# Loading two weight blocks in runs of 1 KB instead of 14 and 7 KB

## The chip, the cores and the metric

The kernel runs on one core of one Trainium2 chip. The metric is device time in microseconds (us) of one execution. The host's work of laying out the inputs before the launch is not part of it. Five engines work side by side: TensorE (PE, matrix multiplications), VectorE (DVE), ScalarE (ACT), GpSimd (POOL) and SyncE (SP, which only issues transfers). Transfers are carried by 16 DMA engines that all queues share. In this kernel nearly all of them are issued by SP (the profile's queue q1); POOL issues some (queue q0), and ACT issues three.

## The reference

The input `A_u` is a sequence of 2048 tokens with 512 features, in bf16. After a layer normalisation the result is a sum of three parts: the input itself, a long convolution and a gated feed-forward block.

```python
xn = _layernorm(x, axis=-1)
return x + _A_ref(xn, ...) + _B_ref(xn, w_gate, w_up, w_down)

# _B_ref
g = jnp.einsum("bsd,df->bsf", x, w_gate)      # 512 -> 1792
u = jnp.einsum("bsd,df->bsf", x, w_up)        # 512 -> 1792
h = _sigmoid(g) * u
return jnp.einsum("bsf,fd->bsd", h, w_down)   # 1792 -> 512
```

`_A_ref` builds, for each of the 512 features, a kernel of length 2048 from 128 complex modes (powers of exp(dt*A), weighted by B and C). It convolves the sequence with it through Fourier transforms of length 4096, and adds the normalised input times `Dskip`.

## The kernel before, in words

The feed-forward block runs in four groups of 512 tokens (L1015). In each group there are 14 column blocks of 128 (`k`, L1021). For each block PE makes the gate product (`fg`, L1027) and the up product (`fu`, L1042) into PSUM banks; ACT takes the sigmoid of the gate (L1036), copies some of the up products to `us_sb` (L1053), and DVE multiplies the two into `hT_sb` (L1057). Then PE multiplies by the down weights (`fd`, L1086).

The convolution needs, first, a ladder of powers, W[0] to W[11], by repeated squaring (L649 to L665). In step k ACT squares both parts (L652), DVE makes the next power (L661, L663), and POOL copies the current power to bf16 with two DMAs (`f_cw`, L655 to L658). The next power is written into one of three buffers in turn. So step k must wait until the copy of step k - 2 has read its buffer (`W_op[-2:-1]`, L664). From the copies, tables of powers are made (`cmul`, lines L718 to L724; `squares`, L771 to L777; seeds copied at L291 or L293). The normalised input is transformed by matrix products (L680 and later). The third and fourth pieces of the input's normalisation take their statistics on ACT or DVE (L531 to L540) and one power function on POOL (L491). Normalised rows of the later groups go out to a scratch (`x_scr`, L568) and return transposed (L570).

The order of the work is written out by hand: `run` (L296) yields the operations in the order of `ORDER`. Each engine and each queue executes its share of that order one after another. The costs and `pkt` values that stand beside operations feed a planner (`_rate`, L306); with `ORDER` written out, they do not move anything.

The weights are loaded once, at the start, by SP, and stay in SBUF: `wg_sb` (gate), `wu_sb` (up) and `wd_sb` (down). By `ORDER`, SP issues at the start: rows 0 and 2 to 3 of the input, the first parameters, a gate piece, input rows 4 to 7, a gate piece, the other parameters, the last gate piece, the first up piece, input rows 12 to 15, the second up piece (L478 with n = 3), input rows 8 to 11, the small table S1 (L475) and the down weights (L484). Then SP comes to the store of the normalised rows 4 to 7 into `x_scr`, for which it waits. Loads on one queue are carried in the order of issue.

The host lays out what is loaded (`_laid_out`, L1149). In the kernel before, each of the 128 partitions finds its part of a weight piece in one run: 7168 bytes of an up piece, 14336 bytes of the down weights.

Of the kernel before, what the change touches and what calls it, by code (L numbers as in the profile page):

```python
# [20 lines left out]
D = 512  # L21
# [4 lines left out]
FT = 14  # L26
# [9 lines left out]
CUT_G = (0, 128, 3 * 128, 7 * 128, 14 * 128)  # L36
CUT_U = (0, 7 * 128, 14 * 128)
# [30 lines left out]
KB = 1024  # L68
# [255 lines left out]
def kernel(  # L324
# [27 lines left out]
    def slots(n):  # L352
        return [_Slot("b") for _ in range(n)]
# [16 lines left out]
    wu_sb = const.tile([128, KT * F], BF, name="wu_sb")  # L370
    wd_sb = const.tile([128, FT, D], BF, name="wd_sb")
# [15 lines left out]
    def at(off, shape, dt=BF):  # L387
        assert off % 32 == 0
        n = int(np.prod(shape)) * (4 if dt == F32 else 2)
        assert off + n <= NBIG, (off, n)  # L390
        v = big[:, off // 2:(off + n) // 2]
        if dt == F32:
            v = v.bitcast(F32)
        if len(shape) > 1:
            ax = ["a%d" % i for i in range(len(shape))]
            v = v.rearrange("p (%s) -> p %s" % (" ".join(ax), " ".join(ax)), **dict(zip(ax[1:], shape[1:])))
        return v
# [21 lines left out]
    def dma(q, dst, src, deps=(), prio=0.0, acq=(), rel=(), pkt=1024, after=None, hv=0.5):  # L419

        n = None
        get = lambda v: v() if callable(v) else v
        holder = {}

        def fn():
            with nc.allow_non_contiguous_dma(reason="laid out"):
                holder["i"] = QUEUE[q].dma_start(out=get(dst), in_=get(src))
            if after:
                after(holder["i"])

        return lambda nbytes: pl.add(q, 0.62, fn, deps, prio, acq, rel, dma=(nbytes, _rate(pkt), hv))
# [8 lines left out]
        return A_u[0:256, :].rearrange("(i p) d -> p i d", i=2)  # L440
    lp = [0.0]

    def load(q, dst, src, nbytes, deps=(), pkt=2048, hv=0.5):
        lp[0] += 0.01
        return dma(q, dst, src, deps=deps, prio=lp[0], pkt=pkt, hv=hv)(nbytes)

    def load_x(i0, n, q="SP"):
        ls = [load(q, xn[:, i0:i0 + n, :], xv(i0, i0 + n), 128 * n * KB,
                   pkt=1024 * n)]
        for i in range(i0, i0 + n):  # L450
            l_x[i] = ls
# [6 lines left out]
    ld, rawn = par[:, 0, :], {nm: par[:, 1 + qi, :] for qi, nm in enumerate(["Are", "Aim", "Bre", "Bim", "Cre", "Cim"])}  # L458
    l_id = None
    l_pa = load("SP", par[:, 0:3, :], A_par[:, 0:3, :], 384 * KB, pkt=3072)  # L460
    l_pbc = load("SP", par[:, 3:7, :], A_par[:, 3:7, :], 512 * KB, pkt=4096)
    l_wg, l_wu = [], []
    piece = lambda k: sum(128 * k >= c for c in CUT_G[1:-1])
# [6 lines left out]
    for n in range(4):  # L470
        fs_ = slice(KT * CUT_G[n], KT * CUT_G[n + 1])
        nb = 1024 * (CUT_G[n + 1] - CUT_G[n])
        l_wg.append(load("SP" if n else "ACT", wg_sb[:, fs_], B_w_gate[:, fs_], nb, pkt=nb // 128))
        if n == 2:
            l_s1 = load("SP", at(OFF["pq"], [128]), cten["S1"].ap(), 32 * KB)  # L475
        if n > 1:
            fs_ = slice(KT * CUT_U[n - 2], KT * CUT_U[n - 1])
            l_wu.append(load("SP", wu_sb[:, fs_], B_w_up[:, fs_], 896 * KB, pkt=7168))  # L478
        if n == 2:
            load_x(4, 4)  # L480
    load_x(8, 4)
    l_dk = load("SP", dskr[0:1, :], A_Dskip.rearrange("(o d) -> o d", o=1), 1 * KB)
    load_x(12, 4)
    l_wd = load("SP", wd_sb[:], B_w_down, 1792 * KB, pkt=14336)  # L484
    l_m2 = load("SP", m2[:], cten["M2"].ap(), 256 * KB, pkt=2048)
    l_sw = load("SP", sw[:], cten["SW"].ap(), 96 * KB, pkt=768)

# [242 lines left out]
    for c in range(4):  # L730
# [10 lines left out]
        n = 1  # L741
# [114 lines left out]
    for p, u2 in [(p, UNITS[p][n:n + 2]) for p in range(NP) for n in range(0, NU // 2, 2)]:  # L856
# [80 lines left out]
        for x, u in enumerate(u2):  # L937
# [6 lines left out]
                               pkt=512)(256 * KB))  # L944
# [34 lines left out]
    for t in range(0, 8, 2):  # L979
        lds = []  # L980
        for n, (p, u0, u1) in enumerate(VPART):
            v_v = v_scr[n][:].rearrange("g (a t r) d -> t (g a) (r d)", a=4, t=4)
            lds.append(dma("SP", vall[16 * u0:16 * u1, t // 2, p], v_v[t // 2],
                           deps=v_st[n] + table_free + z_free * p, prio=20 + n + 0.01 * t, pkt=2048, hv=0.9)(64 * KB * (u1 - u0)))
# [30 lines left out]
    for grp in range(4):  # L1015
        hts, prods = [], []
        for u2 in range(7):
# [3 lines left out]
            for k in (2 * u2, 2 * u2 + 1):  # L1021
                a, b = slots(2)
# [38 lines left out]
        for jj in range(4):  # L1061
# [3 lines left out]
            if jj == 0:  # L1065
                if late:
                    xt = at(TAIL["xt"], [4, D])
                    lx = [dma("SP", xt, xv(i, i + 4), deps=[prods[0]] + table_free, prio=3,
                              pkt=4096)(512 * KB)]
# [30 lines left out]
            if late:  # L1100
# [3 lines left out]
                for (c0, c1), po, my in zip(cols, pos, sums):  # L1104
# [4 lines left out]
                    if jj == 0:  # L1109
                        continue  # L1110
                    q0 = 0 if jj == 1 else r
                    src = lambda r=r, q0=q0, ot=ot, c0=c0, c1=c1: ot()[:, q0:r + 1, c0:c1]
                    dst = outv[:, i - r + q0:i + 1, c0:c1]
                    dma("ACT" if c0 else "SP", dst, src, deps=[fin], prio=1, rel=[osl] if r and c1 == 512 else [],
                        pkt=2 * (c1 - c0))(256 * (c1 - c0) * (r + 1 - q0))
# [23 lines left out]
def _rows(a):  # L1139
    return _swap(a.reshape(2, 32, 2, NT, D).transpose(2, 0, 1, 3, 4).copy()).reshape(128, NT, D)  # L1140
# [4 lines left out]
def _pieces(w, cut):  # L1145
    w = np.asarray(w).reshape(KT, 128, F).swapaxes(0, 1)
    return np.concatenate([w[:, :, a:b].reshape(128, -1) for a, b in zip(cut, cut[1:])], axis=1)

def _laid_out(inputs):  # L1149
    a = dict(inputs)  # L1150
    a['B_w_gate'], a['B_w_up'] = _pieces(inputs['B_w_gate'], CUT_G), _pieces(inputs['B_w_up'], CUT_U)
    a['B_w_down'] = np.asarray(inputs['B_w_down']).reshape(FT, 128, D).swapaxes(0, 1)
    u = _rows(np.asarray(inputs['A_u']))
    a['A_u'] = np.concatenate([u[:, n:m].reshape(-1, D) for n, m in zip(CUT_X, CUT_X[1:])])
    par = [np.asarray(inputs['A_' + n]).T for n in ('A_re', 'A_im', 'B_re', 'B_im', 'C_re', 'C_im')]
    par = np.stack([np.broadcast_to(np.asarray(inputs['A_log_dt']), (NMODE, D))] + par, axis=1)
    a['A_par'] = par.reshape(NMODE, 7, D // 32, 2, 16).swapaxes(3, 4).reshape(NMODE, 7, D)
    return a
# [24 lines left out]
```

## Time and profile before

| | |
|---|---|
| median of three runs | 216.19 us (215.26 to 216.66) |
| the profiled execution | 215.88 us |
| its span, first to last instruction | 214.1 us |
| granted TensorE clock | 0.999 |
| DMA: packets, bytes | 41612, 42.35 MB |

The span is shorter than the execution's time by 1.78 us, which lie before the first and after the last instruction. In the profile's rows, L427 is the line of the helper through which SP and ACT issue their DMAs, and `big` is one large SBUF tile in which many buffers of the convolution live, so it stands for different things in different lines. A row of a timeline has the start and the length in us, the engine, the line, and what is written and read; what stands in brackets is the idle time of the engine ahead of it and what ended that. "DMA to landing" is the time from the issue of a DMA to the moment at which its last byte is reported. A row of a DMA queue gives packets, MB and the time that its packets took as a share of 16 engines over the window asked for.

### The profile page before, as it was taken

The page shows a single profiled execution, that of the slowest core. Times are in us where ns is not written, and L with a number is a line of the kernel's source. Part 1 is how long each engine was busy: PE and PEld are TensorE (multiplying, and loading weights), DVE is VectorE, ACT ScalarE, POOL GpSimd, SP SyncE. Part 2 cuts the span into 40 slices and gives each one's busy share as a digit, 9 for nine tenths or more (in the row PEclk, how much of TensorE's full clock was granted, in tenths as well). Part 3 has the DMA queues.
Part 4 walks back from the last instruction along what each step waited for, and adds up shares of the span by engine and source line. Part 5 has one row for each costly group of instructions (what it writes and reads, how often), then busy time and mean ns, then how long its engine had stood idle before and what let it go on. Part 6 is the DMA issues. An engine that isn't in the chain of part 4 may idle for free.

```text
span 214.1 us, 5720 instructions
## 1 busy us (share of the span) xinstructions
PE 203.1 (95%) x2226; PEld 102.9 (48%) x2251; DVE 196.4 (92%) x423; ACT 175.0 (82%) x359; POOL 33.2 (15%) x66
## 2 busy tenths in 40 slices
PE   7799987999998999999999999999999999999993
PEld 2464433444443444445465565554556546444453
DVE  3999799998999999999999999999999999976863
ACT  3899997999999899898999999979499999732000
POOL 3324025118321000000000003800010000004000
PEclk9999999999999999999999999999999999999999
DMA  6999908952889706598257297580997976989924
GB/s 203 369 421 431 272 6 195 173 86 63 161 232 221 166 5 196 176 210 274 108 165 223 61 267 210 86 123 12 279 294 181 330 229 189 285 242 249 264 108 147
DMA packets 41612, 42.35 MB, mean 198 GB/s; under 512 B 8809, under 2 KB 35058, under 8 KB 41458
## 3 DMA queue, kind: packets, MB, share of 16 engines
q1 hardware_dynamic: 36642, 36.95, 55.2%
q0 software_dynamic: 4512, 4.73, 14.3%
q8 instruction: 17, 0.28, 0.5%
q10 hardware_dynamic: 432, 0.33, 0.5%
q14 instruction: 9, 0.07, 0.1%
HBM read 25.21 MB, written 12.07 MB: 174 GB/s over the span
## 4 chain that ended last, share of the span: by engine, by line
DVE 57%; PE 28%; DMA 6%; ACT 3%; issue 3%; POOL 2%; DVEq 0%; POOLq 0%
DVE big L718 10%; DVE big L719 10%; DVE hT_sb L1057 8%; PE bank L1086 7%; DVE big L723 6%; DVE big L724 6%; PE bank L1027 5%; PE bank L1042 5%; DMA big<-big 4%; PE bank L886 4%; DVE stats L538 2%; DVE big L661 2%; DVE big L663 2%; DVE big L891 2%; PE bank L995 2%
## 5 line engine op out<-in xcount | busy, mean ns | idle before, releaser
L293 ACT ACTIVATE big<-bank 128x512 bf16<-128x512 f32 (+2 forms) x147 | 77.7, 654 | 5.0 <-PE bank L802 3.0
L1027 PE MATMUL bank<-xnT,wg_sb 128*128 128x512 bf16 (+1 forms) x232 | 53.3, 361 | 1.7 <-DVE hT_sb L1057 0.7
L1042 PE MATMUL bank<-xnT,wu_sb 128*128 128x512 bf16 x219 | 52.9, 379 | 1.0 <-DVE hT_sb L1057 0.7
L1086 PE MATMUL bank<-wd_sb,hT_sb 128*128 128x512 bf16 (+1 forms) x230 | 50.3, 366 | 0.7 <-ACT glu_sb L293 0.2
L1036 ACT ACTIVATE hT_sb<-bank 128x512 bf16<-128x512 f32 x56 | 33.3, 648 | 3.4 <-PE bank L1027 3.4
L1086 PEld LDWEIGHTS <-hT_sb 128*128 128x128 bf16 x238 | 22.6, 98 | 26.0 <-issue 2.3
L1027 PEld LDWEIGHTS <-wg_sb 128*128 128x128 bf16 x244 | 22.7, 98 | 25.2 <-issue 4.9
L1042 PEld LDWEIGHTS <-wu_sb 128*128 128x128 bf16 x224 | 21.4, 98 | 27.3 <-issue 3.3
L718 DVE TENSOR_TENSOR big<-big 128x1024 bf16<-128x1024 bf16 (+4 forms) x40 | 27.9, 698 | 0.0
L719 DVE TENSOR_TENSOR big<-big 128x1024 bf16<-128x1024 bf16 (+4 forms) x40 | 27.9, 696 | 0.0
L891 DVE TENSOR_TENSOR big<-big 128x2048 bf16<-128x2048 bf16 x16 | 19.6, 1236 | 0.6 <-ACT big L293 0.4
L1053 ACT ACTIVATE us_sb<-bank 128x512 bf16<-128x512 f32 x29 | 19.2, 667 | 0.7 <-DVE hT_sb L1057 0.7
L886 PE MATMUL bank<-big 128*128 128x256 bf16 x160 | 19.6, 273 | 0.0
L1057 DVE TENSOR_TENSOR hT_sb<-hT_sb,bank 128x512 bf16<-128x512 bf16 x27 | 17.7, 685 | 0.4 <-ACT hT_sb L1036 0.4
L723 DVE TENSOR_TENSOR big<-big 128x512 bf16<-128x512 bf16 (+4 forms) x40 | 17.8, 445 | 0.0
L724 DVE TENSOR_TENSOR big<-big 128x512 bf16<-128x512 bf16 (+4 forms) x40 | 17.8, 444 | 0.0
L886 PEld LDWEIGHTS <-big 128*128 128x128 bf16 x160 | 15.4, 98 | 4.9 <-issue 1.0
L771 ACT ACTIVATE sq_sb<-big 128x256 bf16<-128x256 bf16 (+2 forms) x20 | 14.4, 720 | 3.4 <-DVE big L724 3.4
L657 POOL DMA_DIRECT2D big<-big x24 | 13.0, 547 | 24.9 <-DVE big L663 23.7
L293 ACT ACTIVATE big<-big 128x256 bf16<-128x256 bf16 x31 | 14.7, 485 | 0.4 <-PE bank L802 0.4
L1057 DVE TENSOR_TENSOR hT_sb<-hT_sb,us_sb 128x512 bf16<-128x512 bf16 x29 | 12.3, 434 | 0.0
L652 ACT ACTIVATE big<-big 128x1024 f32<-128x1024 f32 x11 | 11.9, 1078 | 0.0
(99 smaller groups left out, 213.7 us busy)
## 6 DMA issues: line engine op xcount, KB each, us to landing
big<-c_E SPq DMA_DIRECT2D x16, 320.0 KB, 3.9
z_scr<-big SPq DMA_DIRECT2D x16, 256.0 KB, 2.8
big<-z_scr SPq DMA_DIRECT2D x16, 256.0 KB, 4.8
v_scr<-big SPq DMA_DIRECT2D x16, 256.0 KB, 2.9
big<-big POOLq DMA_DIRECT2D x24, 128.0 KB, 3.5
big<-in_A_u_dram SPq DMA_DIRECT2D x4, 512.0 KB, 9.1
big<-v_scr SPq DMA_DIRECT2D x4, 512.0 KB, 4.7
wu_sb<-in_B_w_up_dram SPq DMA_DIRECT2D x2, 896.0 KB, 13.1
```

Of the source, the lines that this page charges most:

```text
L293: nc.scalar.activation(out=get(out), in_=get(in_), func=ACT.Identity)
L718: V.tensor_tensor(out=wide(outp), in0=wide(lo), in1=mre, op=ALU.mult)
L719: V.tensor_tensor(out=wide(tb()), in0=wide(lo), in1=mim, op=ALU.mult)
L723: V.tensor_tensor(out=outp[:, :, 0], in0=outp[:, :, 0], in1=tb()[:, :, 1], op=opr)
L724: V.tensor_tensor(out=outp[:, :, 1], in0=outp[:, :, 1], in1=tb()[:, :, 0], op=opi)
L886: T.matmul(bank(sk[kt == NKT - 1])[:, DW * c:DW * c + DW], es()[:, c, kt, :], kT[p][:, kt, :], start=kt in (0, NKT - 1), stop=kt >= NKT - 2)
L891: V.tensor_tensor(out=pp()[:, :, 0:4, :], in0=xx()[:, :, 0, :].unsqueeze(2).to_broadcast([128, 2, 4, DW]), in1=kb().unsqueeze(1).to_broadc ...
L1027: T.matmul(bank(sl)[:, c0:c1], w_at(w, CUT_G, kt, k), xnT[:, grp, kt, c0:c1], start=(kt == 0), stop=(kt == KT - 1))
L1036: S.activation(out=hT_sb[:, hs.idx, k % 2, :], in_=bank(sl), func=ACT.Sigmoid)
L1042: T.matmul(bank(sl), w_at(wu_sb, CUT_U, kt, k), xnT[:, grp, kt, :], start=(kt == 0), stop=(kt == KT - 1))
L1057: V.tensor_tensor(out=h(), in0=h(), in1=us_sb[:, us.idx, :] if on else bank(sl), op=ALU.mult)
L1086: T.matmul(bank(po)[:, 0:c[1] - c[0]], hT_sb[:, hts[k // 2].idx, k % 2, jj * 128:(jj + 1) * 128], wd_sb[:, k, c[0]:c[1]], start=first and ...
```

## The change

Two weight blocks are laid out otherwise in DRAM, and their loads read them in runs of 1 KB. The down weights keep their natural order (1792 rows of 512); partition p takes the rows p, 128 + p, 256 + p and so on, 14 runs of 1 KB that lie 128 KB apart. The second up piece is laid out as 7 times 128 rows of 512; partition p takes 7 runs of 1 KB, again 128 KB apart. The first up piece keeps its runs of 7 KB. What stands in SBUF afterwards is the same, byte for byte, and so are the number and the order of the DMAs. The default of `pkt` in `load` becomes 1024.

```diff
-    def load(q, dst, src, nbytes, deps=(), pkt=2048, hv=0.5):
+    def load(q, dst, src, nbytes, deps=(), pkt=1024, hv=0.5):
...
             fs_ = slice(KT * CUT_U[n - 2], KT * CUT_U[n - 1])
-            l_wu.append(load("SP", wu_sb[:, fs_], B_w_up[:, fs_], 896 * KB, pkt=7168))
+            rows = B_w_up[896 * (n - 2):896 * (n - 1)]
+            if n == 2:
+                l_wu.append(load("SP", wu_sb[:, fs_], rows.rearrange("(p s) e -> p (s e)", s=7), 896 * KB, pkt=7168))
+            else:
+                l_wu.append(load("SP", wu_sb[:, fs_].rearrange("p (s e) -> p s e", s=7), rows.rearrange("(s p) e -> p s e", s=7), 896 * KB))
...
-    l_wd = load("SP", wd_sb[:], B_w_down, 1792 * KB, pkt=14336)
+    l_wd = load("SP", wd_sb[:], B_w_down.rearrange("(k p) d -> p k d", k=FT), 1792 * KB)
...
-    a['B_w_gate'], a['B_w_up'] = _pieces(inputs['B_w_gate'], CUT_G), _pieces(inputs['B_w_up'], CUT_U)
-    a['B_w_down'] = np.asarray(inputs['B_w_down']).reshape(FT, 128, D).swapaxes(0, 1)
+    a['B_w_gate'], up = _pieces(inputs['B_w_gate'], CUT_G), _pieces(inputs['B_w_up'], CUT_U).reshape(128, 2, 7, 512)
+    a['B_w_up'] = np.concatenate([up[:, 0].reshape(896, 512), up[:, 1].swapaxes(0, 1).reshape(896, 512)])
+    a['B_w_down'] = np.asarray(inputs['B_w_down'])
```

## The prediction

> **What bounds the kernel now.** I read the page's busy shares and its chain of work first, then the same chain in order of time, then VectorE's (DVE's) timeline at the place where that chain leaves an engine, and last the DMA queues in short windows around that place.
>
> ```profile
> span 214.1 us, 5720 instructions
> PE 203.1 (95%) x2226; PEld 102.9 (48%) x2251; DVE 196.4 (92%) x423; ACT 175.0 (82%) x359; POOL 33.2 (15%) x66
> DVE 57%; PE 28%; DMA 6%; ACT 3%; issue 3%; POOL 2%; DVEq 0%; POOLq 0%
> ```
>
> TensorE (PE) and DVE are both nearly full, so there is no idle engine to win from. The chain is 57% DVE, and 6% (about 13 us) is DMA. In order of time the long DMA piece is this:
>
> ```profile
> 17.37 0.75 POOL big L657
> 18.11 9.20 DMA big<-big
> 27.34 0.69 DVE big L661
> ```
>
> It is the first copy of the power ladder (`f_cw`, L657: two DMAs on POOL's queue, W[0] and W[1]). The second of the two lands 9.2 us after its issue, and DVE then goes on. What DVE itself loses there is less, since it has other work until 25.64 (24.96 + 0.68). In its timeline, idle time stands in the brackets:
>
> ```profile
> 24.96 0.68 DVE L1057 TENSOR_TENSOR hT_sb<-hT_sb,bank 128x512 bf16<-128x512 bf16 x1
> 26.83 0.29 DVE L291 COPY big<-big 128x256 bf16<-128x256 bf16 x1 [1.18 <-DMA big<-big]
> 27.34 0.69 DVE L661 SCALAR_TENSOR_TENSOR big<-big 128x512 f32<-128x512 f32 x1 [0.22 <-DMA big<-big]
> ```
>
> So 1.18 + 0.22 = 1.40 us of DVE idle time hang on this copy. Why it is so late shows in the DMA queues: q1 is SP's queue, which at that time carries the down weights; q0 is POOL's, which carries the copies. Two windows, 21.4:23.4 and 20.4:21.4:
>
> ```profile
> DMA packets 96, 0.74 MB, mean 369 GB/s; under 512 B 0, under 2 KB 48, under 8 KB 48
> q1 hardware_dynamic: 48, 0.69, 83.6%
> q0 software_dynamic: 48, 0.05, 14.4%
> ...
> q1 hardware_dynamic: 29, 0.42, 97.7%
> ```
>
> From 21.4 to 23.4 us the two queues take turns one for one: 48 packets of 14 KB against 48 of 1 KB. The second window prices a 14 KB packet: 0.977 x 16 engines x 1.0 us / 29 = 539 ns. A copy packet is priced in 24.0:26.0, when copies run almost alone:
>
> ```profile
> q0 software_dynamic: 367, 0.33, 102.0%
> ```
>
> that is 1.02 x 16 x 2.0 us / 367 = 89 ns. One turn of an engine is thus 539 + 89 = 628 ns, of which 86% is somebody else's packet.
>
> **The change, part by part.** The bytes, the number of DMAs and the order of issue stay. `pkt` enters only the planner's `_rate`; as ORDER is written out, it moves no instruction. What changes is the run length: the down weights (wd) go from 128 runs of 14 KB to 1792 of 1 KB, the second up piece (wu) from 128 runs of 7 KB to 896 of 1 KB.
>
> *The turn gets shorter (the gain).* The only 1 KB runs on q1 beside copies that I can look at are the x_scr store's. Windows 34.3:34.8 (store and copies together) and 35.0:36.2 (store nearly alone):
>
> ```profile
> DMA packets 118, 0.12 MB, mean 240 GB/s; under 512 B 1, under 2 KB 118, under 8 KB 118
> q0 software_dynamic: 63, 0.06, 75.7%
> q1 hardware_dynamic: 55, 0.06, 39.0%
> ...
> q1 hardware_dynamic: 353, 0.36, 99.1%
> ```
>
> Turns are again about one for one (63 to 55), and a 1 KB run costs 0.991 x 16 x 1.2 us / 353 = 54 ns. The first copy is two DMAs of 128 KB in 1 KB packets, 256 packets or 16 on an engine: 16 x (54 + 89) = 2.3 us beside such runs. Landings of L657 in the windows 17:19, 31.5:33 (alone) and 34:37 (beside the store):
>
> ```profile
> DMA to landing us min/median/max: 9.2/9.3/9.4
> ...
> DMA to landing us min/median/max: 2.4/2.7/3.0
> ...
> DMA to landing us min/median/max: 3.5/3.8/4.9
> ```
>
> Earliest landing after the change: 18.1 + 3.0 = 21.1 us. Latest: only the turns already seen shrink. In 21.4:23.4 an engine has 48/16 = 3 turns in 2.0 us, which become 3 x 143 = 0.43 us, so 27.3 - 1.57 = 25.7, plus the 0.87 us by which the wu piece ahead gets longer (below): 26.6. The nearest row is 4.9 us: 18.1 + 4.9 + 0.87 = 23.9, ahead of the 25.64 at which DVE asks. I take the whole wait as gone, **-1.40 us**; at the late end -0.7 us (27.34 - 26.6) would be left of it.
>
> *What is late next.* L661 also needs ScalarE's (ACT's) square, which is ready in time:
>
> ```profile
> 24.38 1.15 ACT L652 ACTIVATE big<-big 128x1024 f32<-128x1024 f32 x1
> ```
>
> After that the other engines must be able to follow a DVE that is 1.40 us earlier. Their next idle times (ACT, then three of PE):
>
> ```profile
> 35.21 0.43 ACT L771 ACTIVATE sq_sb<-big 128x256 bf16<-128x256 bf16 x1 [1.44 <-DVE big L724]
> 29.28 1.89 PE L1042 MATMUL bank<-xnT,wu_sb 128*128 128x512 bf16 x8 [0.36 <-DVE hT_sb L1057]
> 31.48 0.81 PE L1042 MATMUL bank<-xnT,wu_sb 128*128 128x512 bf16 x3 [0.31 <-DVE hT_sb L1057]
> 36.48 0.41 PE L680 MATMUL bank<-big 32*64 32x512 bf16 x6 [1.06 <-ACT us_sb L1053]
> ```
>
> ACT has 1.44 us to give, PE 0.36 + 0.31 + 1.06 = 1.73; both cover 1.40, ACT only just. From 37 us on all engines stand 1.40 us earlier. Nothing later remembers the loads, since the DMA engines are empty meanwhile (columns: PE, PEld, DVE, ACT, POOL busy, clock, DMA share, GB/s):
>
> ```profile
> 28.50:32.50 4.00, 3.33 (x15) 1.35 (x14) 3.93 (x10) 3.97 (x9) 1.51 (x2) 1.00 0.00 0
> ```
>
> Every later transfer is started by an engine, and the order is fixed, so I carry the shift whole to the end.
>
> *More runs (the cost).* A 7 KB run is priced in 16.2:17.4:
>
> ```profile
> q1 hardware_dynamic: 76, 0.51, 101.8%
> ```
>
> 1.018 x 16 x 1.2 / 76 = 257 ns (4 of the 76 are tiny; 72 give 271, which I take). Per engine wu goes from 8 x 271 = 2.17 to 56 x 54 = 3.02 us (+0.87 with unrounded prices), wd from 8 x 539 = 4.31 to 112 x 54 = 6.05 (+1.74): 2.6 us in all. That price is a store's; the change has loads. The ends: 38.5 ns (a KB of a 14 KB run, 539/14; no cost at all) and 89 ns (a copy packet): 168 x 89 = 14.95 us against 6.48, so +8.5 us. I stay at 54, the row with the same queue and size. The cover:
>
> ```profile
> L427 SPq DMA_DIRECT2D wd_sb<-in_B_w_down_dram x1: 328/328/328, 10.3 to 10.3; - x1
> L1086 PE MATMUL bank<-wd_sb,hT_sb x230: 272/379/390, 37.0 to 210.6; 128*128 128x512 bf16 x101, 128*128 128x256 bf16 x14
> DMA to landing us min/median/max: 16.4/16.4/16.4
> ```
>
> The down weights land at 10.3 + 16.4 = 26.7 and are first used at 37.0, or 35.6 after the shift: 8.9 us of cover, more than even the upper end. Between wu and wd on the queue stand x rows 8 to 11, which ACT takes at 25.8, and S1, which PE takes at 35.0 (first two rows below). S1, the last of them, lands at 9.0 + 11.8 = 20.8 us, so 0.87 more is hidden too. Cost on the path: **0**.
>
> ```profile
> 25.80 0.73 ACT L531 ACTIVATE glu_sb<-big 128x512 bf16<-128x512 bf16 x1
> 35.02 0.40 PE L680 MATMUL bank<-big 32*64 32x512 bf16 x2
> ...
> L427 SPq DMA_DIRECT2D big<-c_S x1: 331/331/331, 9.0 to 9.0; - x1
> DMA to landing us min/median/max: 11.8/11.8/11.8
> SPq L427 <- DVE big L552: 22.4, 1, 22.4
> ```
>
> *Issuing.* No row shows SP issuing 1792 runs. It may cost nothing more than today's 0.33 us, or many us; behind wd SP waits 22.4 us for L552 in any case (last row), so I take 0 on the path.
>
> *Sum.* -1.40 + 0 + 0 = -1.40 us. The profiled execution took 215.88 us (214.1 span and 1.78 around it): 214.5. The median of the three runs is 216.19, 0.31 above it: 216.19 - 1.40 = **214.8 us** (-0.65%).
>
> A rule of the Trainium skill speaks against this. "DMA: Bandwidth & Descriptors", section "Queues, rings and completion order", says that an engine switches queues only between packets, and that a packet typically holds some 9 to 17 descriptors. By it the fourteen 1 KB runs of a partition could go out in one turn, and the gain would be none (second rival). The 63 to 55 above disagree with it for this queue, and so do the 48 to 48 for POOL's.
>
> **Rivals.**
>
> *The copies stay late for another reason.* The first copy packets move only at about 21.4, though POOL issued at 17.4 and 18.1: part of the delay is work already queued ahead, not turns. If it grows with the 0.87 us and one engine trails, landing is at 26.6 or later and the gain 0 to 0.7 us: 215.5 to 216.2. For it: L657's second copy, issued at 34.4, also waits behind the store. Against it: even so it needs 4.9 us, and there is 7.5 (25.64 - 18.1).
>
> *The other side: a turn is a whole partition's runs.* Then a turn of the loads becomes 14 x 54 = 756 ns, not 539. An engine has at most 8 such turns of wd, so the copy lands up to 8 x 0.217 = 1.7 us later, and 0.87 for wu: DVE, ACT and PE, with no slack there, end up to 2.6 us later: 216.2 to 218.8, in the middle 217.5. It decides from a turn above 539 ns, ten runs of 54. Against it: 63 to 55.
>
> *The 1 KB loads are much dearer than the store.* wd delays PE once a run costs more than (6.48 + 8.9)/168 = 92 ns; at 110 ns it would be 3.1 us late at L1086, on top of the gain: 217.9.
>
> *More is gained.* DVE's next idle time comes from one POOL instruction of 3.30 us, whose like with the same shape took 1.02:
>
> ```profile
> 48.43 3.30 POOL L491 TENSOR_TENSOR ln_ri<-ln_ve,half 128x4 f32<-128x4 f32 x1 [1.62 <-ACT ln_ve L533]
> 30.99 1.02 POOL L491 TENSOR_TENSOR ln_ri<-ln_ve,half 128x4 f32<-128x4 f32 x1 [9.37 <-DVE ln_ve L540]
> 51.77 0.16 DVE L495 SCALAR_TENSOR_TENSOR ln_nb<-mv,ln_ri 128x4 f32<-128x4 f32 x1 [0.92 <-POOL ln_ri L491]
> ```
>
> If the new timing shortens it, 0.92 more goes: 213.9. Nothing in the change bears on it directly.
>
> **How the numbers follow.** Whole gain 0.70 (214.8; its own range 213.9 to 215.6, as the three runs spread by 0.7 us to either side); copies still late 0.11 (215.9); whole-partition turns 0.07 (217.5); dear loads 0.04 (217.9 and up); more gained 0.08 (213.9 or less). The range from 213.5 to 217.4 leaves out about half of the last three. A measurement of this kernel tells about 1% from no change, that is 214.03 and 218.35. Faster by more: the last case and the lower edge of the first, 0.17. Slower by more: the dear loads and the upper edge of the whole-partition turns, 0.07. Within: 0.76.
>
> **What would show it.** Right: L657's first two landings at 3 to 6 us and not 9; no DMA wait ahead of L291 and L661 near 26 us; L771 at about 33.8 with almost no idle time; the first L1086 at about 35.6; wd landing at about 29.3 on a queue where q0 and q1 take turns one for one at near 54 ns a run. Wrong: landings still above 7.5 us; a wait for wd or wu on PE; or all early marks 1.4 us earlier and the span not, which would mean a wait after 37 us that the shift opens.

## The result, and the profile after

The changed kernel takes 214.55 us (median of 6 runs, 214.19 to 214.88), the kernel before 216.29 us beside it (6 runs). The ratio is 0.9945, with a 95% interval from 0.9922 to 0.9969. That is 1.2 us less, between 0.7 and 1.7. (The two medians lie 1.74 us apart, a little more than the interval allows; the six runs of the kernel before spread over 1.4 us, and the text goes by the recorded ratio.) The forecast was 214.8 us, 0.65% less. The profiled execution takes 214.40 us, its span is 212.7 us; 214.5 and 212.7 were forecast. Lines behind 478 stand 4 lower in the changed kernel: L657 is now L661, and so on.

The changed kernel's timeline of DVE, at the place where it stood idle for 1.40 us:

```profile
25.07 0.68 DVE L1061 TENSOR_TENSOR hT_sb<-hT_sb,bank 128x512 bf16<-128x512 bf16 x1
25.67 0.28 DVE L291 COPY big<-big 128x256 bf16<-128x256 bf16 x1
25.80 0.68 DVE L665 SCALAR_TENSOR_TENSOR big<-big 128x512 f32<-128x512 f32 x1
```

No bracket is left: the copy at L291 starts as soon as L1061 has ended. The first two copies of the ladder (issued at 17.5 and 18.2) now land after:

```profile
DMA to landing us min/median/max: 6.6/6.8/7.0
```

instead of 9.2 to 9.4 us. The queues in the window 22:24 show why:

```profile
DMA packets 507, 0.50 MB, mean 248 GB/s; under 512 B 22, under 2 KB 507, under 8 KB 507
...
q0 software_dynamic: 248, 0.23, 68.4%
q1 hardware_dynamic: 259, 0.27, 47.6%
```

The queues still take turns one for one, but POOL's queue gets 248 packets through in 2.0 us, where it got 48 before. An engine makes 248/16 = 15.5 turns, so a turn is 129 ns instead of 628; 143 was forecast.

The rest of the machine follows (ACT, PE and PE's first product with the down weights):

```profile
33.79 0.42 ACT L775 ACTIVATE sq_sb<-big 128x256 bf16<-128x256 bf16 x1
...
35.05 0.41 PE L684 MATMUL bank<-big 32*64 32x512 bf16 x6 [0.50 <-ACT us_sb L1057]
35.51 0.82 PE L1090 MATMUL bank<-wd_sb,hT_sb 128*128 128x512 bf16 x3
```

ACT's idle 1.44 us are gone, PE waits 0.50 instead of 1.06, and its first product with the down weights starts at 35.5 instead of 37.0. From there to the end both traces run nearly in step: DVE's rows between 56 and 194 us start 1.5 to 1.6 us earlier, and the span is 1.4 us shorter. The chain that ended last now goes through PE:

```profile
PE 55%; DVE 30%; ACT 7%; issue 2%; POOL 2%; DMA 1%; DVEq 0%; ACTq 0%; POOLq 0%
```

DMA has fallen from 6% of the chain to 1%.

The price is paid where it was expected, under cover:

```profile
L427 SPq DMA_DIRECT2D wd_sb<-in_B_w_down_dram x1: 461/461/461, 13.8 to 13.8; - x1
DMA to landing us min/median/max: 15.8/15.8/15.8
```

The down weights land at 29.6 us (26.7 before; 29.3 forecast), and nothing uses them before 35.5.

### The profile page after: what moved, and what is told of

Same layout as the page of the kernel before. It is cut to its first block, busy times and chain, and to the rows that moved or that the text cites. A ratio compares the mean times of both kernels' runs of the same rounds, so it can differ in the third digit from the quotient of the medians.

```text
span 212.7 us, 5745 instructions
## 1 busy us (share of the span) xinstructions
PE 205.2 (96%) x2251; PEld 103.2 (49%) x2251; DVE 196.2 (92%) x423; ACT 174.8 (82%) x359; POOL 33.0 (16%) x66
## 3 DMA queue, kind: packets, MB, share of 16 engines
q1 hardware_dynamic: 39074, 36.95, 56.8%
## 4 chain that ended last, share of the span: by engine, by line
PE 55%; DVE 30%; ACT 7%; issue 2%; POOL 2%; DMA 1%; DVEq 0%; ACTq 0%; POOLq 0%
PE bank L1090 15%; PE bank L1031 11%; PE bank L1046 10%; PE bank L890 8%; DVE hT_sb L1061 5%; ACT big L293 4%; DVE big L667 3%; DVE big L665 3%; DVE stats L542 3%; DVE big L723 2%; DVE big L722 2%; PE bank L923 2%; PE bank L806 2%; PE bank L874 2%; DVE big L604 2%
## 5 line engine op out<-in xcount | busy, mean ns | idle before, releaser
L1031 PE MATMUL bank<-xnT,wg_sb 128*128 128x512 bf16 (+1 forms) x244 | 54.1, 362 | 1.1 <-DVE hT_sb L1061 0.7
L1090 PE MATMUL bank<-wd_sb,hT_sb 128*128 128x512 bf16 (+1 forms) x238 | 50.9, 367 | 0.3 <-ACT glu_sb L293 0.2
L1090 PEld LDWEIGHTS <-hT_sb 128*128 128x128 bf16 x238 | 22.5, 98 | 25.9 <-issue 2.3
L1031 PEld LDWEIGHTS <-wg_sb 128*128 128x128 bf16 x244 | 22.7, 98 | 25.2 <-issue 4.9
L1046 PEld LDWEIGHTS <-wu_sb 128*128 128x128 bf16 x224 | 21.4, 98 | 26.3 <-issue 2.1
L722 DVE TENSOR_TENSOR big<-big 128x1024 bf16<-128x1024 bf16 (+4 forms) x40 | 27.2, 679 | 0.0
L723 DVE TENSOR_TENSOR big<-big 128x1024 bf16<-128x1024 bf16 (+4 forms) x40 | 27.0, 676 | 0.0
L1061 DVE TENSOR_TENSOR hT_sb<-hT_sb,bank 128x512 bf16<-128x512 bf16 x27 | 17.7, 684 | 0.4 <-ACT hT_sb L1040 0.4
L727 DVE TENSOR_TENSOR big<-big 128x512 bf16<-128x512 bf16 (+4 forms) x40 | 17.0, 425 | 0.0
L728 DVE TENSOR_TENSOR big<-big 128x512 bf16<-128x512 bf16 (+4 forms) x40 | 17.0, 424 | 0.0
L661 POOL DMA_DIRECT2D big<-big x24 | 13.0, 546 | 24.6 <-DVE big L667 23.4
L775 ACT ACTIVATE sq_sb<-big 128x256 bf16<-128x256 bf16 (+2 forms) x20 | 14.3, 715 | 2.0 <-DVE big L728 2.0
L1061 DVE TENSOR_TENSOR hT_sb<-hT_sb,us_sb 128x512 bf16<-128x512 bf16 x29 | 12.0, 424 | 0.0
```

Source lines behind the costliest of these rows:

```text
L722: V.tensor_tensor(out=wide(outp), in0=wide(lo), in1=mre, op=ALU.mult)
L723: V.tensor_tensor(out=wide(tb()), in0=wide(lo), in1=mim, op=ALU.mult)
L727: V.tensor_tensor(out=outp[:, :, 0], in0=outp[:, :, 0], in1=tb()[:, :, 1], op=opr)
L1031: T.matmul(bank(sl)[:, c0:c1], w_at(w, CUT_G, kt, k), xnT[:, grp, kt, c0:c1], start=(kt == 0), stop=(kt == KT - 1))
L1046: T.matmul(bank(sl), w_at(wu_sb, CUT_U, kt, k), xnT[:, grp, kt, :], start=(kt == 0), stop=(kt == KT - 1))
L1061: V.tensor_tensor(out=h(), in0=h(), in1=us_sb[:, us.idx, :] if on else bank(sl), op=ALU.mult)
```

## The experiments

The theory is that the length of q1's turns makes the ladder's first copies late, and that the change gains what DVE waits for them and nothing else. Its rivals: the gain comes from the up piece, or from something other than that wait. "Wait" in the table is DVE's idle time ahead of L291 and L661 (L665) near 26 us; "last landing" is the issue of the second of the first two copies plus its time to landing, worked out from rounded rows ("under" where nothing waited and only a bound can be given). "Weights" is the landing of the down weights.

| kernel | first issue | wait | last landing | weights | span | ratio to before (interval) |
|---|---|---|---|---|---|---|
| before, as profiled above | 17.4 | 1.40 | 27.3 | 26.7 | 214.1 | |
| before, once more (e9) | 17.8 | 0.98 | 27.4 | 26.5 | 214.3 | 0.9986 (0.9967 to 1.0005) |
| the changed kernel | 17.5 | 0 | under 25.3 | 29.6 | 212.7 | 0.9945 (0.9922 to 0.9969) |
| down weights alone, 1 KB (e1) | 17.4 | 0 | under 25.4 | 29.3 | 212.7 | 0.9947 (0.9926 to 0.9967) |
| up piece alone, 1 KB (e2) | 17.6 | 1.70 | 27.8 | 27.1 | 214.9 | 1.0026 (1.0011 to 1.0042) |
| down weights, 7 KB (e3) | 17.9 | 0.32 | 26.8 | 26.4 | 213.6 | 1.0001 (0.9983 to 1.0018) |
| the same again (e10) | 17.4 | 1.36 | 27.4 | 27.1 | 214.6 | 1.0014 (0.9996 to 1.0033) |
| down weights, 2 KB (e4) | 17.7 | 0 | under 26.2 | 29.8 | 213.1 | 0.9963 (0.9948 to 0.9978) |
| both, 512 B (e5) | 17.4 | 0.29 | 26.2 | 30.6 | 213.0 | 0.9958 (0.9936 to 0.9981) |
| before, wait filled (e6) | 17.4 | 0 | 27.1 | 26.3 | 212.7 | 0.9936 (0.9909 to 0.9964) |
| before, two edits of the order (e12) | 17.5 | 0 | 26.9 | 25.9 | 211.8 | 0.9903 (0.9880 to 0.9925) |

**e1: the down weights alone.** The kernel before, with one of the two layouts:

```diff
-    l_wd = load("SP", wd_sb[:], B_w_down, 1792 * KB, pkt=14336)
+    l_wd = load("SP", wd_sb[:], B_w_down.rearrange("(k p) d -> p k d", k=FT), 1792 * KB)
```

> Only the down weights in 1 KB runs; the second up piece keeps its 7 KB runs. Theory (the length of the turns of the down weights makes the ladder's first copies late): the copies land by about 25 us, DVE waits 0 to 0.2 us near 26 us instead of 1.40, and the time is that of the changed kernel, 0.994 of before (about 1.3 us less). Rival (the gain comes from the up piece: its 896 runs hold SP back, so that the down weights are issued at 13.8 us and not at 10.3): without them SP issues the down weights at 10.3 again, the copies land at 26.8 and 27.3, the wait of 1.40 us stays and the time is 1.00 of before.

Time 214.31 us, ratio 0.9947; no wait. SP issued the down weights at 10.0 us, so holding SP back plays no part. The down weights alone carry the gain.

**e2: the up piece alone.** The changed kernel with the down weights as before.

> Only the second up piece in 1 KB runs; the down weights keep their 14 KB runs. Theory: the turns stay at about 628 ns, the copies land at 27 us or up to 0.9 us later, DVE waits 1.4 to 2.3 us, the time is 1.000 to 1.004 of before. Rival (SP held back by the up piece): the down weights are issued at about 13.8 us, the copies land before 25.7 us and the time is 0.994 of before.

Here SP does issue the down weights at 13.9 us, and yet:

```profile
27.30 0.29 DVE L291 COPY big<-big 128x256 bf16<-128x256 bf16 x1 [1.47 <-DMA big<-big]
27.81 0.69 DVE L665 SCALAR_TENSOR_TENSOR big<-big 128x512 f32<-128x512 f32 x1 [0.23 <-DMA big<-big]
```

The wait grows by 0.30 us, and the kernel is 0.26% slower than before (216.16 us). This half of the change does not help: alone it loses, and with the other half it adds nothing that shows (0.9945 with it, 0.9947 without it in e1).

**e3 and e10: runs of 7 KB.** The down weights in two runs of 7 KB per partition:

```diff
+    l_wd = load("SP", wd_sb[:].rearrange("p (j a) d -> p j (a d)", a=7), B_w_down.rearrange("(j p) e -> p j e", j=2), 1792 * KB)
```

> Only the down weights changed, to two runs of 7 KB per partition. A turn is 269 + 89 = 358 ns instead of 628. Theory in its simple form (wait in proportion to the turn): the copies land about 1.2 us earlier, the wait falls from 1.40 to 0.2 to 0.7 us, time 0.996 to 0.998. Rival within the theory (a copy that is not through when the down weights are finished ends when the rest of the down weights and its own 16 packets are through, whatever the turn): about 4.3 packets of 14 KB are left on an engine at 21.4 us, that is 2.3 us, and 16 copy packets 1.4 us, so the end is 25.1 us on an average engine for 14 and for 7 KB alike; the landings stay near 27 us, the wait at 1.0 to 1.4 us and the time at 0.999 to 1.00.

In the first run the wait was only 0.32 us, but the ladder had started 0.5 us late, and the time had not moved. So the kernel was run again:

> The down weights in runs of 7 KB once more. In the first look the copies landed 8.2 us after their issue (before: 9.2 to 9.4), the wait was 0.32 us, but DVE itself was 0.5 us late for another reason, and the time was 1.000 of before with an interval of 0.2% to either side. If the shorter turn is worth what the landing shows (1.1 us of 1.4), the wait ahead of L291 and L661 is 0.3 to 0.5 us and the time 0.995 to 0.997; if the early delay comes with this kernel, it shows again, and the time stays at 0.998 to 1.000.

```profile
25.81 0.28 DVE L291 COPY big<-big 128x256 bf16<-128x256 bf16 x1
27.46 0.69 DVE L661 SCALAR_TENSOR_TENSOR big<-big 128x512 f32<-128x512 f32 x1 [1.36 <-DMA big<-big]
...
L427 SPq DMA_DIRECT2D wd_sb<-in_B_w_down_dram x1: 389/389/389, 9.8 to 9.8; - x1
DMA to landing us min/median/max: 17.3/17.3/17.3
```

Halving the turn moves the first of the two copies (L291 hardly waits), not the second, for which L661 waits 1.36 us. The second landed at 26.8 us in one execution and 27.4 in the other (27.3 and 27.4 with 14 KB), and the time is that of before in both runs. So the wait does not go with the length of the turn. The expectation's second form holds: a copy that is not through when the down weights are finished ends when the rest of them and its own packets are through, and that is the same amount of work for 14 and 7 KB. (The 25.1 us worked out there are for an average engine; which engines trail, and why, the trace does not name.) The table bears this out, and it accounts for the difference between e3 and e10: in the seven traces with runs of 7 or 14 KB the copies land 0.3 to 1.0 us behind the down weights, in e3 (26.4 and 26.8) as in e10 (27.1 and 27.4). With packets of 1 or 2 KB they land at least 3.6 us ahead of them. Only turns so short that all 16 fit in before the down weights are finished bring the landing forward.

**e4: runs of 2 KB.** As e3, with `a=2` and `j=7`.

> Only the down weights changed, to seven runs of 2 KB per partition. A turn is about 84 + 89 = 173 ns, 16 turns 2.8 us from about 21.5 us. Both forms of the theory: the copies land near 24.4 us on an average engine and by 25.4 us on the last, DVE waits 0 to 0.3 us, the time is 0.994 to 0.996 of before, as with 1 KB runs. If only runs of 1 KB and less take turns one for one, landings stay above 26 us.

No wait, 214.87 us, ratio 0.9963. The span is 0.4 us longer than with 1 KB alone, and 0.3 of that is the later start of the ladder (17.7 against 17.4). Both forms of the theory said this; the one of e10 says the rest as well.

**e5: both blocks in runs of 512 bytes.**

> Both blocks in runs of 512 bytes, twice as many runs as in the changed kernel. On the gain: turns of about 27 + 89 = 116 ns, the copies land no later than in the changed kernel, no wait on DVE. On the cost: 112 + 224 runs on an engine at 27 to 40 ns are 9 to 13.4 us instead of 9.1, so the down weights land between 29.6 and about 34 us, still before 35.5 us where PE needs them: time equal to the changed kernel within 0.3 us (0.994 of before). If loads in short runs are dear (over 54 ns a run of 512 bytes), PE waits at its first product with the down weights. On the start of the copies, 4 us after their issue in both kernels: if a fixed number of runs goes ahead of them, they land 1 us or more earlier than the 6.6 to 7.0 us of the changed kernel; if a fixed amount of data or time does, at 6 us or more.

The down weights landed at 17.1 + 13.5 = 30.6 us, and PE did not wait for them. But the copies landed later than in the changed kernel (7.3 to 8.0 us after their issue), and 0.29 us of wait came back. The window 22:24 shows that the down weights did not move in 512 bytes:

```profile
q1 hardware_dynamic: 194, 0.40, 59.2%
q0 software_dynamic: 189, 0.18, 52.6%
```

0.40 MB in 194 packets are 2 KB each, though the layout has runs of 512. So this was another test of 2 KB, with the up piece alone in packets of 512 bytes. SP's queue carried 39074 packets, as many as in the changed kernel, so neither the cost of more packets nor the question of what goes ahead of the copies was answered by it.

**e6: long runs, the wait filled.** The kernel before, with two products moved in `ORDER`:

```diff
-    191, 671, 115, 658, 630, 62, 643, 667, 668, 113, 649, 112, ...
+    643, 649, 191, 671, 115, 658, 630, 62, 667, 668, 113, 112, ...
```

> The kernel before with its long runs; only two entries of the written-out order are moved: the two products of L1057 that DVE makes at 28.55 us go ahead of the copy at L291 and the power at L661, so that DVE works (1.2 us) while it waits for the ladder's copies. Theory (the change gains what DVE waits, and nothing else): the copies still land about 9 us after their issue, the wait falls from 1.40 to 0.2 to 0.5 us, and the time falls by 0.9 to 1.2 us, to 0.995 of before. Rival (the shorter turns help by something else than this wait, or the wait has cover further down): 1.00 of before.

```profile
25.02 1.87 DVE L1057 TENSOR_TENSOR hT_sb<-hT_sb,bank 128x512 bf16<-128x512 bf16 x3
26.81 0.28 DVE L291 COPY big<-big 128x256 bf16<-128x256 bf16 x1
27.10 0.69 DVE L661 SCALAR_TENSOR_TENSOR big<-big 128x512 f32<-128x512 f32 x1
```

The copies land as late as ever (8.9 to 9.0 us after their issue), DVE works meanwhile, and the time is 214.52 us, ratio 0.9936. The wait is gone whole, where 0.2 to 0.5 us of it was expected to stay. The interval takes in the changed kernel's ratio. So the gain is this wait, and the rival that shorter turns help elsewhere falls.

**e9: the kernel before once more.**

> The kernel before, unchanged, for a second profile of it and to see how far two equal kernels differ: ratio 1.000 within 0.2%. In the first profile the early parameter load landed at 6.3 us, in the looks at the other kernels up to 1.1 us later, which delayed the start of the ladder by up to 0.5 us. If this is a matter of the single execution, this profile has it too at times; the wait ahead of L291 and L661 should be 1.4 us within 0.3.

```profile
26.72 0.28 DVE L291 COPY big<-big 128x256 bf16<-128x256 bf16 x1 [0.62 <-DMA big<-big]
27.37 0.69 DVE L661 SCALAR_TENSOR_TENSOR big<-big 128x512 f32<-128x512 f32 x1 [0.36 <-DMA big<-big]
```

The parameters landed later in this execution, and the first copies were issued 0.46 us later. The last copy landed at the same 27.4 us, so the wait was 0.98 us. The wait of the kernel before soaks up what comes late ahead of it. Without the wait such a delay seems to go through to the end, as in e4; no run was made to show this.

**e8: does DVE hold the copies back?** The changed kernel, with a statistics step moved to the moment of the copies' issue.

> The changed kernel, with DVE's statistics of one token tile (about 1.0 us, one SBUF input, tiny output) moved from just ahead of the products of L1057/L1061 to the moment at which POOL issues the first two copies (17.4 us); the issue of one input load moves up in the text only. It asks why the copies' first packets move only 4 us after their issue in every kernel so far, whatever the run length. If DVE's products of two SBUF inputs, which run back to back from 17.1 us, keep POOL from writing the transfers' descriptors, that 1.0 us lets them through, and the first copies land 4.5 to 5.5 us after their issue instead of 6.6 to 7.0. If what is queued on the DMA engines sets the delay, the landings stay at 6.5 us or more. The time should be that of the changed kernel within 0.3%, since DVE does the same work.

They landed after 6.6 to 7.0 us, as in the changed kernel; 214.50 us, ratio 0.9948 (0.9926 to 0.9970). So keeping DVE's products of two inputs away for 1.0 us at the first issue does not bring the copies forward.

**e7 and e11: the next wait.** The changed kernel has 0.92 us of DVE idle time left near 50 us, behind POOL's power function. First the small product that needs it was moved back by four DVE instructions:

> The changed kernel with one entry of the order moved: DVE's small product after POOL's power function (the 0.92 us of idle time near 50 us) goes behind the next step of the ladder and one sum, which need nothing from POOL. If a DVE wait here is worth as much as the one near 26 us: 0.9 us less than the changed kernel, 0.990 of before. If ACT or PE set the pace from 50 us on: no change against the changed kernel, 0.994 of before. I expect between: the wait gone, 0.3 to 0.9 us less.

```profile
50.74 0.27 DVE L728 TENSOR_TENSOR big<-big 128x256 bf16<-128x256 bf16 x1
51.94 0.16 DVE L499 SCALAR_TENSOR_TENSOR ln_nb<-mv,ln_ri 128x4 f32<-128x4 f32 x1 [0.92 <-POOL ln_ri L495]
```

The wait moved along, to the hundredth: the function took 4.85 us instead of 3.21 and ended 0.9 us after DVE had run out of work. Time 214.79 us, ratio 0.9950 (0.9930 to 0.9971): nothing. Then more work went ahead of it:

```diff
-    73, 104, 76, 105, 707, 77, 79, 234, 150, 167, 705, 109, ..., 235, 194, 770, 108, 107, 147, 746, 747, 106,
+    73, 76, 104, 707, 77, 234, 79, 150, 167, 705, ..., 235, 194, 770, 147, 746, 747, 105, 109, 108, 107, 106,
```

> The changed kernel; the small DVE product and the normalisation that wait for POOL's power function near 50 us go behind more of DVE's other work, up to the first product that reads PSUM (L1061), and POOL makes the ladder's copy ahead of the power function. In the kernel with one entry moved the function simply took 1.6 us longer and ended 0.9 us after DVE had run out of work, so DVE's products seem to hold it back. Theory (it gets on beside products that read PSUM, as the second one did near 30 us in 1.02 us): the wait falls to 0 to 0.5 us, and the time is 0.2 to 0.8 us under the changed kernel's. Rival (it needs DVE idle for about 0.9 us wherever it stands): the wait of 0.9 us stays, only later, and the time is the changed kernel's.

DVE no longer waits, and the time is 213.40 us, ratio 0.9901 (0.9870 to 0.9932), against 214.50 us for e8 on the same chip. This beats the kernel before, and by 1.1 us also e8, whose work is that of the changed kernel (runs of 213.29 to 214.37 against 214.24 to 215.78). But the reason was not the one expected. The next rows are DVE's and POOL's in e11:

```profile
50.50 0.27 DVE L728 TENSOR_TENSOR big<-big 128x256 bf16<-128x256 bf16 x1
50.81 0.69 DVE L722 TENSOR_TENSOR big<-big 128x1024 bf16<-128x1024 bf16 x1
51.42 0.69 DVE L723 TENSOR_TENSOR big<-big 128x1024 bf16<-128x1024 bf16 x1
...
48.09 3.57 POOL L495 TENSOR_TENSOR ln_ri<-ln_ve,half 128x4 f32<-128x4 f32 x1
```

The function ends at 51.66, ahead of the PSUM product. It needed neither that nor an idle DVE of 0.9 us: a gap of 0.04 us (50.77 to 50.81) was enough, and it ended 0.89 us after that gap began. (The trace of e12, below, has the same: a gap from 50.98 to 51.02 us, and the function ends at 51.86.)

**e12: the order alone.** The kernel before with its long runs, and the edits of e6 and e11.

> The kernel before, with its runs of 14 and 7 KB, and the two edits of the order put together: the two products go ahead of the waiting copy and power near 26 us, and the work that waits for the power function near 50 us goes later. If run length matters only through the DVE wait near 26 us, this equals the changed kernel with the second edit (0.990 of before, about 213.4 us), although the copies still land about 9 us after their issue. If the shorter runs have a worth of their own, it stays above that by 0.3% or more, at 0.993 to 0.996.

213.58 us, ratio 0.9903, with the copies landing 8.5 to 8.6 us after their issue. Two edits of the order do without the layout what e11 does with it; the shorter runs have no other worth that these runs can show.

## Why the prediction was right

*The wait goes.* Right: 1.40 us of idle time near 26 us became 0, and the profiled span fell by 1.4 us; the step that had waited starts at 25.80 instead of 27.34. e6 shows that this is the whole of it.

*The landing.* The term was mis-sized: it took the nearest row, 4.9 us, and put the landing at 23.9. Measured were up to 7.0 us, that is up to 25.2, which left 0.5 us before DVE's demand at 25.67, where 1.7 had been counted on. The upper bound of 26.6 holds. Why the row beside the store was too short a measure was not tested. That the first packets move only some 4 us after the issue was named in the first rival, and that part of it was true. What saved the sum is that the 16 turns then took only some 2.1 us on average (16 x 129 ns). With 0.5 us to spare, that the whole wait went was partly luck.

*Why the landing moves.* The step by which the 3 turns that an engine has in 21.4:23.4 become 0.43 us put the lateness down to turns alone. By that, 7 KB runs would have won more than half of it; e3 and e10 show that they win nothing measurable. The turns did halve (below); what the step left out is that the copies must get all their turns in before the long load is finished.

*One for one.* Right. The rule weighed in the prediction, from the Trainium skill, "DMA: Bandwidth & Descriptors", section "Queues, rings and completion order" (9 to 17 descriptors go out before a switch), is not what this trace shows: 259 runs of 1 KB stood against 248 copy packets. Equal counts alone could also come from equal batches, but the packets' start times in the traces leave only turns of one: the most frequent time from one copy packet to a later one is 620 to 630 ns with runs of 14 KB, 350 to 360 with 7, 170 to 180 with 2 and 130 to 140 with 1, against 70 to 80 where copies run almost alone (24.3:26 of the kernel before). These are the turns of 628, 358, 173 and 143 ns that were worked out ahead. The turn of 129 is under 54 + 89 because the two packets' times overlap: the shares in 22:24 add up to 116%. The rival built on it (216.2 to 218.8 us) is out.

*The cost, zero on the path.* Right. The price of a run was forecast at 54 ns, from a store. In the window 20.6:21.5, with loads nearly alone,

```profile
q1 hardware_dynamic: 305, 0.30, 103.6%
```

it is 1.036 x 16 x 0.9 / 305 = 49 ns (10 of the 305 are tiny). The up piece's longer queue is not worth nothing in every setting, though: with long turns behind it, it cost 0.26% (e2).

*The other engines follow.* Right: L775 at 33.79 (33.8 forecast), the first L1090 at 35.51 (35.6).

*More is gained.* Did not happen by itself: the power function took 3.21 us instead of 3.30, and the wait of 0.92 us stayed. e11 shows that the gain was there to be had by an edit of the order.

*The measured 1.2 us against 1.40.* The interval holds both. The absolute forecast of 214.8 started from 216.19, a median of three; on the chips of the experiments the kernel before had medians of 215.57 to 215.67, so its closeness to 214.55 says less than the ratio does. That the wait of the kernel before is shorter when the ladder starts late (0.98 us in e9) would make the gain less than 1.40 in such executions; how often they start late was not measured.

## What to carry to other kernels

Look at who waits for a small transfer, and at the size of the packets that another queue sends at the same time: here long runs were cheap for the load itself (539 ns for 14 KB, against 49 for each KB in short ones) and dear for whoever had to take turns with it (628 against 129 ns a turn). Shortening them paid only once all of the small transfer's turns fitted in before the long load was finished: 2 KB sufficed and 7 KB did not. And before a layout is changed, see whether the waiting engine has other work to put into the gap: two entries of the order did the same.

## What the runs showed of the hardware

**A load of many runs holds back the next issue.** SP's timeline in the changed kernel:

```profile
6.58 0.39 SPq L427 DMA_DIRECT2D wu_sb<-in_B_w_up_dram  x1
7.72 4.85 SPq L427 DMA_DIRECT2D big<-in_A_u_dram  x1
12.62 1.15 SPq L427 DMA_DIRECT2D big<-c_S  x1
```

Behind the up piece's 896 runs the next issue takes 4.85 us, where it took 0.33 before; with 512-byte runs it takes 8.12 us. SP had nothing else to do here. A queue with an urgent small transfer behind such a load would feel it.

**A start that the run length does not change.** In the window 20.6:21.5 above, the profile lists no packet of POOL's queue, though POOL issued at 17.5 us. The first copies land 6.6 to 7.1 us after their issue with 1 KB runs, of which the turns take 2.1 us; alone they land after 2.4 to 3.0. Turns do not explain the difference, and in e8 keeping DVE's products away for 1.0 us changed nothing. The packets' start times say a little more: in all fourteen traces the first copy packet moves 4.0 to 4.3 us after the first issue, whether that is at 17.4 us (the kernel before) or at 17.9 (e3), and whether the down weights were issued at 9.6 us (e12) or at 17.1 (e5). Where the copies run alone it moves 1.1 us after the issue (33.1 after 32.0 us in the kernel before). So the start follows POOL's issue and not the issue of the load ahead of it. What the 4 us beside a busy SP queue are spent on stays open.

**POOL gets in at DVE's gaps.** POOL's power function reads two SBUF operands, and so do the DVE products beside it. It took 1.02 us near 30 us, but 2.83 (e8) to 4.85 (e7) near 50, where in the kernels before and after, e6 to e8, e11 and e12 it ended 0.9 us after the first moment at which DVE paused: 0.9 us of idle time in e7, a gap of 0.04 us in e11. This agrees with the Trainium skill, "SBUF — State Buffer", section "Who interferes with whom": a DVE instruction with two SBUF inputs contends with a GpSimd instruction that reads SBUF, and the ports that the two engines share are "an exclusive lock". That the gap in e11 is what let it in was read from the times, not tried separately.
